# Six more fillers ahead of the first hash, and a hash of two query columns moved behind the first turns

## The chip, the cores and the metric

The kernel runs on one core of a Trainium2 chip. The core has five engines that run side by side and wait for each other by semaphores: TensorE (PE, with PEld for its weight loads), VectorE (DVE), ScalarE (ACT), GpSimd (POOL) and SyncE (SP, which issues DMAs here). TensorE writes to PSUM, which DVE and ACT read. The metric is the device time in microseconds of one execution; the median of several runs is compared.

## The reference

Hashed attention, then a gated feed-forward layer:

```python
q_bits = (np.einsum('bhsd,dk->bhsk', q, proj) > 0).astype(np.int64)
k_bits = (np.einsum('bhsd,dk->bhsk', k, proj) > 0).astype(np.int64)
q_bucket = np.sum(q_bits * powers, axis=-1)          # and k_bucket
mask = q_bucket[:, :, :, None] == k_bucket[:, :, None, :]
scores = np.where(mask, scale * np.matmul(q, k.transpose(0, 1, 3, 2)), -1000000000.0)
attn = softmax(scores)                                # over the keys
x = np.matmul(attn, v), as (4*768, 512)
out = x + sigmoid(x @ w_res) * (gelu(x @ w_gate) * (x @ w_val) @ w_out)
```

There are 4 batches of 8 heads, 768 positions, 64 dimensions, 6 hash bits, and a hidden width of 1536. A query attends only to keys in the same bucket of the 6-bit hash.

## The kernel before, in words

Two heads make a pair, so there are 16 pairs, four to a batch. A loaded pair of queries or keys is a tile of 128 partitions by 12 columns of 64 numbers; a column is a set of 128 positions, columns 0 to 5 belong to the first head and 6 to 11 to the second.

For each pair the queries and keys are prepared. `cast` (L255 to L265) writes them as bf16 into a tile `nat`, 128 wide per column: 64 values, then room for 6 bits, then a constant. `tr` (L269 to L274) transposes the loaded numbers in blocks of 32 on DVE into `t32`. For pair 0 `hash_one` (L311 to L320) multiplies `t32` by the projection, in two fp32 matmuls per call, which the profile shows as four instructions at L319; `bits_one` (L322 to L327) transposes the sums in PSUM on DVE (L324) and writes the signs as bits into `nat` (L326). `turn_pe` (L366 to L374) turns columns of `nat` by TensorE transposes into PSUM, one tile under the tag "f" for keys and one under "r" for queries, and `turned` (L376 to L382) copies them to `aug` on ACT (L380) or DVE (L382). With the bits as further rows of `aug`, one matmul gives scores that are far lower where the buckets differ.

`scores` (L494 to L513) computes a chunk of 1024 scores per partition, in a tile `sp` of the pool `sc_ps`, which has two buffers of two PSUM banks each, and takes the exponential on ACT (L512). `values` (L467 on) multiplies the exponentials with the values. A batch ends in `gate_val` and `project`, the feed-forward part, which is spread over the next batch's attention.

The order of the work in batch 0 is written out by hand in the list PLAN (L17 to L76). Lines L727 and L728 call each step in turn. Each engine carries out its own instructions in that order, and waits only for what its next instruction needs; so the list sets an order per engine, and no time. The names of steps: ('tr', pair, side, first column, last), side 0 being the queries and 1 the keys; ('hash1', ..., place); ('bits1', ...); ('turn', ..., tag); ('copy', ..., engine) is `turned`; ('S', chunk) is `scores`; ('va', pair) and ('vs', pair) prepare values on POOL; ('load', pair, side) is issued by SP; ('fill', n, columns) is `fill`.

`fill` (L227 to L229) issues matmuls of a constant into the tile `wps` (L223), whose results are used by nothing. `wps` is taken from `sc_ps` before the first score chunk. The hashes with the places 'w1' and 'w0' also use it: keys 2 to 5 in its second bank, queries 4 and 5 in its first (L313 to L315). The places 'av' are tiles of another pool. The score chunk 0 takes the other buffer of `sc_ps`, chunk 1 the one that `wps` had.

The core of the list at the place of the change, ahead of the first score chunk: fillers (4 + 44 + 4); hash of queries 0 to 3, of keys 0 and 1, of keys 2 to 5, of queries 4 and 5; turns of keys 0 and 1 and of queries 0 to 3; hash of queries 6 to 11; turns of keys 2 to 5 and of queries 4 and 5; chunk 0. Between them stand the steps of DVE, ACT and POOL.

Of the kernel before, what the change touches and what calls it, by code (L numbers as in the profile page):

```python
# [9 lines left out]
FP32 = mybir.dt.float32  # L10
# [7 lines left out]
    ('load', 1, 0), ('load', 1, 1), ('load_v', 0), ('load', 2, 0), ('load_v', 1), ('load', 2, 1),  # L18
    ('load', 3, 0), ('proj', 's', 'pssp'), ('proj', 'w', 'pppp'), ('cast', 0, 1, 'p', 0, 6),
# [73 lines left out]
def kernel(  # L93
# [17 lines left out]
    P = 128  # L111
# [37 lines left out]
    sc_ps = ctx.enter_context(tc.tile_pool(name="sc_ps", bufs=2, space=PSUM))  # L149
# [70 lines left out]
            else:  # L220
                eng.tensor_copy(dst(a), projn)

    wps = sc_ps.tile([P, 1024], FP32, tag="sp", name="wps")  # L223

    ones = nc.const_aps.tensor(1.0, [P, 1], BF16)

# [15 lines left out]
    for s in range(3):  # L242
        n = KF // 3
# [11 lines left out]
    def cast(p, side, eng, c0=0, c1=HT):  # L255
        x = (p, side)
        scale = (1.0 / C) if side == 0 else 1.0
        sl = slice(c0, c1)
        dst = nat_of(x)[:, sl, 0:D]
        if eng is nc.scalar:  # L260
            nc.scalar.activation(dst, raw[x][:, sl], AF.Copy, scale=scale)
        elif side == 0:
            eng.tensor_scalar(dst, raw[x][:, sl], scale, 1.0, op0=ALU.mult, op1=ALU.mult)  # L263
        else:
            eng.tensor_copy(dst, raw[x][:, sl])  # L265

    t32, hsum, htok = {}, {}, {}
# [43 lines left out]
    def hash_one(p, side, c0, c1, tag):  # L311
        n, x = c1 - c0, (p, side, c0)
        if tag in ("w0", "w1"):  # L313
            a = 512 * int(tag[1])
            hsum[x] = wps[:, a:a + 2 * n * 32].rearrange("p (i c n) -> p i c n", i=2, c=n)  # L315
        else:
            hsum[x] = (av_ps if tag == "av" else mm_ps).tile([P, 2, n, 32], FP32, tag=tag, name="hs1")
        for dh in range(2):
            nc.tensor.matmul(hsum[x][:, 0], projs[:, dh, :], t32[p, side][:, c0:c1, dh, :],  # L319
                             start=(dh == 0), stop=(dh == 1))  # L320
# [45 lines left out]
    def turn_pe(p, side, c0, c1, tag, pool=mm_ps):  # L366
        x = (p, side)
        if x not in aug:
            aug[x] = aug_pool.tile([P, HT, P], BF16, tag=f"aug{side}", name=f"aug{side}")
        k = (p, side, c0 // T)  # L370
        if k not in pts:
            pts[k] = pool.tile([P, T, P], BF16, tag=tag, name="pt")
        for c in range(c0, c1):
            nc.tensor.transpose(pts[k][0:KA, c % T, :], nat_of(x)[:, c, 0:KA], ident)  # L374

    def turned(p, side, c0, c1, eng):  # L376
        dst = aug[p, side][0:KA, c0:c1, :]
        pt = pts[p, side, c0 // T][0:KA, c0 % T:c0 % T + c1 - c0]
        if eng is nc.scalar:
            nc.scalar.activation(dst, pt, AF.Copy)  # L380
        else:
            eng.tensor_copy(dst, pt)  # L382
# [321 lines left out]
    def first_gv(i):  # L704
# [7 lines left out]
            [ENG[e] for e in engs]),  # L712
        cast=lambda p, side, e, *c: cast(p, side, ENG[e], *c),
        hash1=hash_one,
        bits1=bits_one,
        turn=lambda p, side, c0, c1, tag: turn_pe(p, side, c0, c1, tag, POOLS[tag]),
        copy=lambda p, side, c0, c1, e: turned(p, side, c0, c1, ENG[e]),
# [3 lines left out]
        va=vals_a, vs=vals_s, finish=finish, open=opened, preset=preset, repeat=repeat,  # L721
# [11 lines left out]
    for s in range(NSLOT, LAST):  # L733
        p, c = divmod(s, NCH)
# [60 lines left out]
```

## Time and profile before

| what | us |
|---|---|
| median of 3 runs | 341.46 |
| the three runs | 341.46, 339.53, 341.53 |
| the profiled execution's own time | 341.21 |
| its span in the trace | 339.2 |
| PE busy | 331.7 |
| DVE busy | 216.4 |
| ACT busy | 214.1 |
| POOL busy | 175.0 |

The span runs from the first to the last instruction in the trace; the execution's own time holds some 2 us more. A row of a timeline gives start, length, engine, line, operation, what is written and read, the number of instructions merged into the row, and in brackets how long the engine was idle before it and what ended that. Merged matmuls overlap, so that a row can end after the next one starts; the time from one row's start to the next one's is the better measure of pace. A row of the list of waits gives the engine and line that waited, what released it, the total in us, the number of times and the longest. The chain is the work that ended last, followed back from the end.

### The profile page before, as it was taken

The page shows a single profiled execution, that of the slowest core. Times are in us where ns is not written, and L with a number is a line of the kernel's source. Part 1 is how long each engine was busy: PE and PEld are TensorE (multiplying, and loading weights), DVE is VectorE, ACT ScalarE, POOL GpSimd, SP SyncE. Part 2 cuts the span into 40 slices and gives each one's busy share as a digit, 9 for nine tenths or more (in the row PEclk, how much of TensorE's full clock was granted, in tenths as well). Part 3 has the DMA queues.
Part 4 walks back from the last instruction along what each step waited for, and adds up shares of the span by engine and source line. Part 5 has one row for each costly group of instructions (what it writes and reads, how often), then busy time and mean ns, then how long its engine had stood idle before and what let it go on. Part 6 is the DMA issues. An engine that isn't in the chain of part 4 may idle for free.

```text
span 339.2 us, 7693 instructions
## 1 busy us (share of the span) xinstructions
PE 331.7 (98%) x3039; PEld 206.2 (61%) x3086; DVE 216.4 (64%) x458; ACT 214.1 (63%) x247; POOL 175.0 (52%) x260
## 2 busy tenths in 40 slices
PE   8999999999999999999999999999999999999996
PEld 8677665565666655555566665666565665666444
DVE  6877765656377977877477896886478444434243
ACT  4799982227999962337999983245999994322220
POOL 4579940233379962477789981667979100000000
PEclk9999999999999999999999999999999999999999
DMA  7996999999966324527057942925050340000012
GB/s 216 376 278 115 240 212 204 184 142 197 309 211 166 97 84 96 94 48 176 12 141 236 248 132 85 141 46 96 1 124 34 79 100 33 31 2 0 31 64 94
DMA packets 74387, 43.88 MB, mean 129 GB/s; under 512 B 52544, under 2 KB 71360, under 8 KB 74352
## 3 DMA queue, kind: packets, MB, share of 16 engines
q1 hardware_dynamic: 67872, 37.95, 45.0%
q0 software_dynamic: 6400, 5.44, 10.7%
q8 instruction: 24, 0.39, 0.4%
q14 instruction: 11, 0.09, 0.1%
q10 hardware_dynamic: 80, 0.00, 0.0%
HBM read 29.56 MB, written 6.29 MB: 106 GB/s over the span
## 4 chain that ended last, share of the span: by engine, by line
PE 82%; POOL 8%; ACT 4%; DVE 3%; DMA 2%; issue 2%; POOLq 0%; DVEq 0%; ACTq 0%
PE sp L526 36%; PE fps L572 14%; PE sp L501 14%; PE av L476 7%; PE rps L558 5%; POOL pr L336 4%; PE hs L284 3%; ACT ering L512 3%; PE hs L319 1%; ACT e L512 1%; PE pt L374 1%; POOL v L395 1%; DMA x_sb<-x_tok 1%; DMA ld<-in_q_dram 1%; DVE sums L342 1%
## 5 line engine op out<-in xcount | busy, mean ns | idle before, releaser
L512 ACT ACTIVATE e<-sp 128x1024 bf16<-128x1024 f32 x117 | 117.7, 1027 | 8.6 <-PE sp L501 3.5
L336 POOL TENSOR_TENSOR pr<-ld,projr 128x384 f32<-128x384 f32 x96 | 93.9, 997 | 47.1 <-DVE sums L342 32.7
L543 ACT ACTIVATE gt<-sp 128x768 bf16<-128x768 f32 x48 | 38.9, 810 | 83.7 <-PE sp L526 80.0
L501 PE MATMUL sp<-aug,aug 71*128 71x256 bf16 (+1 forms) x384 | 86.0, 326 | 0.5
L572 PE MATMUL fps<-wo,hh 128*128 128x512 bf16 (+2 forms) x287 | 74.5, 361 | 1.3
L546 DVE TENSOR_TENSOR hh<-gt,sp 128x768 bf16<-128x768 bf16 x48 | 45.8, 954 | 42.9 <-PE sp L526 39.5
L526 PE MATMUL sp<-x_sb,wg 128*128 128x512 bf16 (+1 forms) x377 | 70.6, 325 | 0.4
L526 PE MATMUL sp<-x_sb,wv 128*128 128x512 bf16 (+1 forms) x374 | 70.4, 325 | 0.5
L476 PEld LDWEIGHTS <-e 128*128 128x128 bf16 x936 | 43.6, 97 | 25.9
L342 DVE TENSOR_REDUCE sums<-pr 128x6 f32<-128x384 f32 x96 | 50.2, 542 | 10.7 <-POOL pr L336 10.4
L526 PEld LDWEIGHTS <-wg 128*128 128x128 bf16 x384 | 37.1, 98 | 25.8 <-issue 1.5
L526 PEld LDWEIGHTS <-wv 128*128 128x128 bf16 x384 | 37.5, 98 | 24.9 <-issue 0.2
L476 PE MATMUL av<-va,e 128*128 128x65 bf16 x936 | 47.0, 193 | 0.2
L572 PEld LDWEIGHTS <-hh 128*128 128x128 bf16 x312 | 28.2, 98 | 21.5
L501 PEld LDWEIGHTS <-aug 71*128 71x128 bf16 x384 | 29.3, 97 | 11.5 <-issue 2.7
L575 DVE SCALAR_TENSOR_TENSOR fps<-th,fps 128x512 f32<-128x512 f32 (+2 forms) x26 | 17.0, 653 | 25.9 <-PE fps L572 25.8
L512 ACT ACTIVATE ering<-sp 128x1024 bf16<-128x1024 f32 x27 | 25.8, 1031 | 1.7 <-PE sp L501 1.4
L558 PE MATMUL rps<-wr,x_sb 128*128 128x512 bf16 x91 | 26.0, 379 | 0.2
L562 ACT ACTIVATE th<-rps 128x512 f32<-128x512 f32 x24 | 14.3, 594 | 18.7 <-PE rps L558 17.5
L273 DVE STREAM_TRANSPOSE t<-ld 128x768 f32<-128x768 f32 (+3 forms) x28 | 23.0, 842 | 0.8 <-PE hs L284 0.6
L455 DVE COPY av<-av 128x390 f32<-128x390 f32 x24 | 13.6, 566 | 14.6 <-PE av L451 14.5
L263 POOL TENSOR_SCALAR nat<-ld 128x768 bf16<-128x768 f32 (+1 forms) x12 | 9.6, 805 | 19.1 <-DMA aug<-nat 17.2
(72 smaller groups left out, 261.7 us busy)
## 6 DMA issues: line engine op xcount, KB each, us to landing
ldv<-in_v_dram SPq DMA_DIRECT2D x16, 384.0 KB, 5.4
out_dram<-o SPq DMA_DIRECT2D x23, 256.0 KB, 2.1
ld<-in_q_dram SPq DMA_DIRECT2D x15, 384.0 KB, 6.2
ld<-in_k_dram SPq DMA_DIRECT2D x15, 384.0 KB, 5.5
wg<-in_moe_w_gate_dram POOLq DMA_DIRECT2D x4, 384.0 KB, 8.6
wv<-in_moe_w_val_dram POOLq DMA_DIRECT2D x4, 384.0 KB, 10.1
wo<-in_moe_w_out_dram POOLq DMA_DIRECT2D x3, 512.0 KB, 7.2
wr<-in_moe_w_res_dram POOLq DMA_DIRECT2D x1, 512.0 KB, 15.5
```

Of the source, the lines that this page charges most:

```text
L273: nc.vector.transpose(t32[p, side][:, sl].rearrange("p c h n -> p (c h n)"), raw[p, side][:, sl].rearrange("p c d -> p (c d)"))
L336: nc.gpsimd.tensor_mul(pr, raw[x][:, hi * T:(hi + 1) * T], projr[:, bit].unsqueeze(1).to_broadcast([P, T, D]))
L342: nc.vector.reduce_sum(sums[x][:, hi * T:(hi + 1) * T, bit], pr, axis=mybir.AxisListType.X)
L476: nc.tensor.matmul(av[p, hi][:, qt, :], e[:, off:off + P], va[:, hi, jt, 0:D + 1], start=first, stop=(repeats(p, hi) and jt == T - 1), ski ...
L501: nc.tensor.matmul(sp[:, off:off + nq * P], ks[0:KA, hi * T + jt, :], qs[0:KA, hi * T + qt0:hi * T + qt0 + nq, :], start=True, stop=True)
L512: nc.scalar.activation(e, sp, AF.Exp, scale=float(ALPHA))
L526: nc.tensor.matmul(sp[:, c0:c1], w[:, kk, bass.ts(m, P)], xs[:, kk, c0:c1], start=(kk == 0), stop=(kk == KM - 1))
L543: nc.scalar.activation(gt, sp[:, 0:S], AF.Gelu)
L546: nc.vector.tensor_mul(hidden[b][:, m, :], gt, ps[1][:, 0:S])
L558: nc.tensor.matmul(rps, x_sb[b][:, kk, t, :], wr[:, kk, :], start=(kk == 0), stop=(kk == KM - 1))
L572: nc.tensor.matmul(fps[:, cs], hh[:, m, bass.ts(t, P)], wo[:, m, cs], start=(m == 0), stop=(m == KF - 1))
L575: nc.vector.scalar_tensor_tensor(fps[:, cs], th[:, cs], 1.0, fps[:, cs], op0=ALU.add, op1=ALU.mult)
```

## The change

Three things change. The second group of fillers has 50 instead of 44. The pool `sc_ps` gives a second tile `wpt` beside `wps`, and the hash of keys 2 to 5 ('w1') now stands at the beginning of `wps`, that of queries 4 and 5 ('w0') at the beginning of `wpt`; score chunk 0 then takes the buffer of `wps` and chunk 1 that of `wpt`. And in the list, the hash of queries 4 and 5 stands behind the first two turns instead of ahead of them. On each of DVE, ACT, POOL and SP the order of instructions is the same as before.

```diff
-    ... ('tr', 0, 0, 4, 6), ('fill', 44, 64),
+    ... ('tr', 0, 0, 4, 6), ('fill', 50, 64),
...
-    ('hash1', 0, 1, 2, 6, 'w1'), ('hash1', 0, 0, 4, 6, 'w0'), ('tr', 0, 0, 6, 12),
-    ('turn', 0, 1, 0, 2, 'f'), ('copy', 0, 1, 0, 2, 's'), ('bits1', 0, 1, 2, 6), ('load', 3, 1),
-    ('bits1', 0, 0, 4, 6), ('turn', 0, 0, 0, 4, 'r'), ('va', 0), ('tr', 0, 1, 6, 12),
+    ('hash1', 0, 1, 2, 6, 'w1'), ('tr', 0, 0, 6, 12), ('bits1', 0, 1, 2, 6),
+    ('turn', 0, 1, 0, 2, 'f'), ('copy', 0, 1, 0, 2, 's'), ('turn', 0, 0, 0, 4, 'r'), ('hash1', 0, 0, 4, 6, 'w0'), ('load', 3, 1),
+    ('bits1', 0, 0, 4, 6), ('va', 0), ('tr', 0, 1, 6, 12),
...
-    wps = sc_ps.tile([P, 1024], FP32, tag="sp", name="wps")
+    wps, wpt = [sc_ps.tile([P, 1024], FP32, tag="sp", name=name) for name in ("wps", "wpt")]
...
-            a = 512 * int(tag[1])
-            hsum[x] = wps[:, a:a + 2 * n * 32].rearrange("p (i c n) -> p i c n", i=2, c=n)
+            hsum[x] = (wpt, wps)[int(tag[1])][:, 0:2 * n * 32].rearrange("p (i c n) -> p i c n", i=2, c=n)
```

2 rows, old and new, of the table PLAN are left out of this document.

## The prediction

> **What bounds the kernel now.** I read the page first (busy time, chain), then the chain in order of time over the first 50 us, then the timelines of PE, PEld, DVE and ACT over the first 12 us with shapes kept apart, and last the waits from 10.5 us on.
>
> ```profile
> span 339.2 us, 7693 instructions
> ...
> PE 331.7 (98%) x3039; PEld 206.2 (61%) x3086; DVE 216.4 (64%) x458; ACT 214.1 (63%) x247; POOL 175.0 (52%) x260
> ...
> PE 82%; POOL 8%; ACT 4%; DVE 3%; DMA 2%; issue 2%; POOLq 0%; DVEq 0%; ACTq 0%
> ```
>
> PE is busy for 98% of the span and carries 82% of the chain. Work that moves off PE's way near the start moves the end only if PE, and what follows it closely, comes out earlier. So the question is when PE finishes the preparation of pair 0. The chain says what that stretch is made of (start, length, what):
>
> ```profile
> 3.42 0.46 DVE t L273
> 3.88 0.14 issue
> 4.01 1.94 PE hs L319 x8
> 5.95 1.71 PE wps L319 x8
> 7.66 0.64 PE pt L374 x6
> 8.30 1.35 PE hs L319 x4
> 9.64 0.34 PE pt L374 x6
> ```
>
> From 4.01 us on there is nothing but PE in it, back to back. The reader should compare the two rows of six transposes: the same instructions take 0.64 us, then 0.34 us. PE's own timeline shows the same for other forms:
>
> ```profile
> 0.85 2.93 PE L229 MATMUL wps<-const-bfloat16-1.0 128*128 128x64 bf16 x52 [0.85 <-PEq L779]
> 4.01 1.94 PE L319 MATMUL hs<-t,projs 128*128 128x128 f32 x8 [0.24 <-DVE t L273]
> 5.74 1.92 PE L319 MATMUL wps<-t,projs 128*128 128x128 f32 x8
> 7.45 0.85 PE L374 MATMUL pt<-ident,nat 128*71 128x128 bf16 x6
> 8.09 1.55 PE L319 MATMUL hs<-t,projs 128*128 128x192 f32 x4
> 9.48 0.50 PE L374 MATMUL pt<-ident,nat 128*71 128x128 bf16 x6
> 9.82 1.23 PE L501 MATMUL sp<-aug,aug 71*128 71x512 bf16 x5
> 10.88 0.81 PE L319 MATMUL hs<-t,projs 128*128 128x192 f32 x4
> 11.53 0.50 PE L374 MATMUL pt<-ident,nat 128*71 128x128 bf16 x6
> ```
>
> Start to start (next row's start less this one's), four 192-column hash matmuls take 9.48 - 8.09 = 1.39 us and later 11.53 - 10.88 = 0.65; six transposes 8.09 - 7.45 = 0.64 and later 9.82 - 9.48 = 0.34. So PE goes at half pace until about 9.48 and at full pace from there. The page's PEclk reads 9 throughout and does not show it; the rows do. There is one break before: PE waits 0.24 us for DVE's first transpose, ahead of 4.01.
>
> **The change, part by part.**
>
> *Six more fillers.* Their weight loads and the next one's:
>
> ```profile
> 0.81 2.80 PEld L229 LDWEIGHTS <-const-bfloat16-1.0 128*128 128x128 bf16 x52 [0.81 <-issue]
> 3.98 1.78 PEld L319 LDWEIGHTS hs<-t,projs 128*128 128x128 f32 x8 [0.37 <-POOL projs L221]
> ```
>
> 52 in 2.80 us is 0.054 each; six are 0.32 us. PEld is idle for 0.37 us before 3.98. The last filler's load then ends at 0.81 + 2.80 + 0.32 = 3.93, ahead of 3.98, so the first hash should start where it does: cost 0, cover the 0.37 us of waiting for DVE's transpose. If that cover shrinks (the first half of the queries landing earlier), at most the whole 0.32 us goes onto the path. The six close the break on PE nearly completely (0.05 us is left).
>
> *The two hashes get a buffer each.* DVE's timeline (its own order is the same after the change, so are those of ACT, POOL and SP's loads: of the moved steps only the hash and the turns are PE's, and they change places with each other):
>
> ```profile
> 5.99 0.27 DVE L324 STREAM_TRANSPOSE hs<-hs 128x64 f32<-128x64 f32 x1 [0.20 <-PE hs L319]
> 6.29 0.17 DVE L326 TENSOR_SCALAR nat<-hs 128x12 bf16<-128x12 f32 x1
> 6.38 0.57 DVE L273 STREAM_TRANSPOSE t<-ld 128x384 f32<-128x384 f32 x1
> 7.70 0.33 DVE L324 STREAM_TRANSPOSE wps<-wps 128x128 f32<-128x128 f32 x1 [0.75 <-PE wps L319]
> 8.06 0.18 DVE L326 TENSOR_SCALAR nat<-wps 128x24 bf16<-128x24 f32 x1
> 8.28 0.27 DVE L324 STREAM_TRANSPOSE wps<-wps 128x64 f32<-128x64 f32 x1
> 8.58 0.17 DVE L326 TENSOR_SCALAR nat<-wps 128x12 bf16<-128x12 f32 x1
> 8.67 0.57 DVE L273 STREAM_TRANSPOSE t<-ld 128x384 f32<-128x384 f32 x1
> 9.98 0.42 DVE L382 COPY aug<-pt 71x512 bf16<-71x512 bf16 x1 [0.75 <-PE pt L374]
> ```
>
> The bits of keys 2 to 5 (7.70) wait 0.75 us until all eight matmuls into wps are done (5.74 + 1.92 = 7.66), though their own four come first. With a tile of their own they can start when DVE is free, 6.38 + 0.57 = 6.95. But who waits for them? The turn of keys 2 to 5, at 9.48, that is 1.24 us after 8.06 + 0.18 = 8.24. At the pace of before this gain is worth nothing on the path.
>
> *The hash of queries 4 and 5 behind six transposes.* Nothing is added, PE's work only changes order. The turns of keys 0, 1 need the bits that end at 6.29 + 0.17 = 6.46; PE finishes its third hash's issue near 6.6 (half of the 1.71 us between 5.74 and 7.45), so no wait at the old pace. The hash ends 0.64 us later, at 8.30; bits 8.28 to 8.75 take 0.47, so they end at 8.8; their turn follows four transposes behind 9.48: a margin of 0.7 us, covered by the 1.39 us hash of columns 6 to 11. Cost 0; without that cover 0.47 us and more. The second score buffer is taken until 8.8, and the second score chunk wants it after 10 us: no wait. Each queue that steps are moved past (SP's load of pair 3's keys, POOL's values of pair 0) keeps its order.
>
> *What is left is the pace.* PE went to full pace after 9.48 - 4.01 = 5.47 us of unbroken work; the fillers before the break did not bring it. If it is unbroken work that counts, and the break is closed, the count starts at 0.85 and full pace comes at 0.85 + 5.47 = 6.3 us. Then, in the new order: rest of the third hash to 6.55; six transposes 0.34, to 6.9; the moved hash at half of its 0.86, to 7.3; columns 6 to 11, 0.65, to 8.0; six transposes, to 8.3: first scores at about 8.35 instead of 9.82, 1.45 us earlier. DVE has to keep up: the moved hash's last result stands at about 7.6, its bits at 8.1, needed at 8.2 by the last two transposes: just in time. In the old order and tile these would stand the same 0.1 us from the edge, so the reorder adds little by itself. DVE next does 0.57 us of transposing, to 8.67, then the copy that stood at 9.98: 1.3 us earlier.
>
> I take that the time is kept to the end, less a little: DVE's 1.3 and PE's 1.45 bound it from below and above at this turning point, and an earlier one (right at the first hash, 4.0) saves up to half of 9.48 - 4.0, cut by DVE's chain (rows 5.99 to 8.75, work of 0.27 + 0.17 + 0.57 + 0.33 + 0.18 + 0.27 + 0.17, that PE's clock does not shorten) to about 2. [...]
>
> What could be late next is data. From 10.5 to 50 us the list of waits, 17 entries, begins
>
> ```profile
> POOL nat L305 <- DVE ht L296: 4.3, 2, 2.5
> DVE rec L420 <- PE av L448: 3.8, 1, 3.8
> DVE aug L382 <- PE pt L374: 2.5, 2, 2.0
> ```
>
> and names no DMA at all: no engine waits there for a load. One load is tight before it:
>
> ```profile
> 9.66 0.82 POOL L387 CAST va<-ldv 128x768 bf16<-128x768 f32 x1 [1.29 <-DMA ldv<-in_v_dram]
> ...
> 15.42 0.65 PE L476 MATMUL av<-va,ering 128*128 128x65 bf16 x16
> ```
>
> It does not move, but its first reader, at 15.42, has 4.9 us to spare after 10.48. So I take the whole gain as kept.
>
> The sum: fillers 0, buffers 0, reorder 0, pace -1.3 to -2.0, I take -1.55, a little beyond the two figures at 6.3 since some executions will turn earlier. The profiled execution took 341.21 us (span 339.2 and 2.0 around it), 0.25 under the median of 341.46; against its own time 339.7, against the median 339.9. The three runs before are 341.46, 339.53 and 341.53: one of them already stands 1.9 us under the others, which is what an earlier turn of the pace would look like. I read it so, but no trace of that run is there.
>
> **Rivals.**
>
> *The pace turns when it did.* The break of 0.24 us may not be what decides: what counts could be how densely PE is filled, and the first hashes may be too thin whatever stands ahead of them. Then only the hidden reorderings remain: 341.4 us, 341.2 to 341.6. For it: 2.93 us of fillers alone had not raised the pace. Against it: the stretch from 5.74 to 9.48 is made of the same kinds of hash and of transposes, and at its end the pace rose. [...]
>
> *More than that.* Keys 2 to 5 being free 0.75 us earlier matters more at full pace than I reckon, and the turn comes near 4.3 in most runs: 2.4 us, 339.0. Against: the same chain of DVE.
>
> *Slower: the fillers hold up the first hash.* Place: PE between last filler and first hash. By the rows 0.05 us are left. Once DVE's transpose ends more than 0.05 us sooner than 3.42 + 0.46 = 3.88, each filler stands in the way; the price is at most 0.32 us, on the path one to one, with the pace turning as late as before: 341.8 us. It decides where that transpose starts before about 3.37 us.
>
> **How the numbers follow.** The earlier turn 0.62 (339.9, own range 339.3 to 340.4), no earlier turn 0.20 (341.4), more 0.08 (339.0), slower 0.10 (341.8). The predicted time is that of the first. The range takes in the other cases with some 0.4 us of scatter below: 338.6 to 341.9. A measurement of this kernel can tell about 1% from no change, 3.4 us: under 338.05 or over 344.87. No case reaches either: half the slow stretch is 2.7 us at the very most, and the fillers cost 0.3. I leave 0.03 on the fast and 0.04 on the slow side for something unseen, such as a wait that the new order brings; 0.93 for within 1%.
>
> **What would show it.** Right: 58 fillers ending near 3.93, no idle row before the first hash, which still starts near 4.0; the first six transposes already at about 0.05 us each; DVE's 128x128 transpose of wps at about 6.95 with no wait for the later hash; first scores near 8.4 and the first exponential 1.4 us earlier than 10.45:
>
> ```profile
> 10.45 3.99 ACT L512 ACTIVATE ering<-sp 128x1024 bf16<-128x1024 f32 x4
> ```
>
> Wrong: transposes still at 0.107 us each before 9 us (no earlier turn), the first hash near 4.3 (held up), PE idle before the turns, or a load that becomes the end of a wait between 8 and 25 us (gain given back).

## The result and the profile after

Over 22 runs each the changed kernel takes 340.96 us (340.35 to 341.74) and the kernel before 339.49 us (338.97 to 341.53): ratio of the means 1.0033, interval 1.0021 to 1.0046. The change makes it slower, by a third of a per cent (the medians differ by 0.43%). The forecast was 339.9 us, a gain.

One thing about the base has to be said first. Of the three runs of before that were known, 341.46, 339.53 and 341.53, two belong to the slower of two groups, and so does the profiled one, 341.21. All 138 runs of its code that were taken here fall into two groups (one of 345.95 is left out): 94 at 338.67 to 340.04, 44 at 341.01 to 341.59. The first group is called the usual kind below, the second the later kind; the trace of before is of the later kind.

The page of the changed kernel shows six matmuls and six weight loads more, and a span 0.6 us shorter than that of the trace of before. The last line is one of the DMA queues: packets, MB, share.

```profile
span 338.6 us, 7705 instructions
...
PE 329.7 (97%) x3045; PEld 203.9 (60%) x3092; DVE 216.3 (64%) x458; ACT 213.8 (63%) x247; POOL 175.3 (52%) x260
...
q8 instruction: 24, 0.39, 0.5%
```

PE's timeline at the start (one line number less than before throughout):

```profile
0.85 3.25 PE L229 MATMUL wps<-const-bfloat16-1.0 128*128 128x64 bf16 x58 [0.85 <-PEq L778]
3.98 1.11 PE L318 MATMUL hs<-t,projs 128*128 128x128 f32 x8
4.92 0.66 PE L318 MATMUL wps<-t,projs 128*128 128x128 f32 x4
5.80 0.50 PE L373 MATMUL pt<-ident,nat 128*71 128x128 bf16 x6 [0.21 <-DVE nat L325]
6.13 0.61 PE L318 MATMUL wpt<-t,projs 128*128 128x64 f32 x4
6.58 0.87 PE L318 MATMUL hs<-t,projs 128*128 128x192 f32 x4
7.30 0.76 PE L373 MATMUL pt<-ident,nat 128*71 128x128 bf16 x6
7.89 1.23 PE L500 MATMUL sp<-aug,aug 71*128 71x512 bf16 x5
```

There is no break ahead of the first hash any more, it starts at 3.98 as before (4.01), and full pace is there from the first hash on: six transposes take 6.13 - 5.80 = 0.33 us, where the first six of before took 0.64. The first scores stand at 7.89 instead of 9.82. DVE's rows show the hash of keys 2 to 5 released by itself, at 6.07, instead of at 7.70 after the later hash; and PE now waits 0.21 us ahead of the turns, for the bits of keys 0 and 1, with the moved hash queued behind them.

```profile
5.48 0.17 DVE L325 TENSOR_SCALAR nat<-hs 128x12 bf16<-128x12 f32 x1
5.57 0.58 DVE L273 STREAM_TRANSPOSE t<-ld 128x384 f32<-128x384 f32 x1
6.07 0.29 DVE L323 STREAM_TRANSPOSE wps<-wps 128x128 f32<-128x128 f32 x1
```

So the start is 1.93 us earlier than in the trace of before. Set side by side, the exponentials keep 1.93 us until 110 us and 1.90 until the end of batch 1. Three of the last ones there, before and after:

```profile
119.48 3.25 ACT L512 ACTIVATE e<-sp 128x1024 bf16<-128x1024 f32 x3
```

```profile
117.58 3.25 ACT L511 ACTIVATE e<-sp 128x1024 bf16<-128x1024 f32 x3
```

Then comes the feed-forward part of batch 1. PE's first matmuls that need the last part of `x_sb`, before and after:

```profile
128.48 0.48 PE L526 MATMUL sp<-x_sb,wg 128*128 128x512 bf16 x2
```

```profile
127.90 0.48 PE L525 MATMUL sp<-x_sb,wg 128*128 128x512 bf16 x2 [1.37 <-DMA x_sb<-x_tok]
```

Of the 1.90 us, 0.58 are left, and they stay 0.55 to 0.58 to the end. PE waits 1.37 us for the DMA that transposes `x_tok`. SP's rows for the store ahead of it and for the transpose, before and after:

```profile
125.00 0.36 SPq L580 DMA_DIRECT2D out_dram<-o  x1
125.70 1.21 SPq L429 DMA_TRANSPOSE x_sb<-x_tok  x1
```

```profile
123.13 0.35 SPq L579 DMA_DIRECT2D out_dram<-o  x1
123.82 2.27 SPq L428 DMA_TRANSPOSE x_sb<-x_tok  x1
```

Times of landings and of single packets stand in the trace, not in the views shown. By the landings the store took 127.16 - 123.13 = 4.03 us instead of 2.06, the transpose 127.86 - 123.82 = 4.04 instead of 2.74. No load runs beside them. Busy time in three stretches of after (the last two numbers are the DMA share and GB/s):

```profile
122.00:123.00 1.00, 1.00 (x7) 0.59 (x6) 0.96 (x2) 0.98 (x2) 0.55 (x1) 1.00 0.00 0
...
125.00:126.00 1.00, 1.00 (x7) 0.45 (x5) 0.00 (x0) 0.00 (x0) 0.00 (x0) 1.00 2.34 132
126.00:127.00 1.00, 0.53 (x3) 0.13 (x2) 0.36 (x1) 0.00 (x0) 0.00 (x0) 1.00 0.08 22
```

Ahead of the store nothing moves (0 GB/s); from 125 to 126 us the packets stand waiting (a share of 2.34 at 132 GB/s), and from 126 to 127 hardly anything moves, though the transpose is not done. One packet is there that belongs to no transfer of the program. Queue q8 carries instructions, 0.39 MB in 24 packets of 16 KB each; it is taken for PE's, since PE has 6137 of the 7705 instructions (matmuls and weight loads) and the next engine on the page, DVE, has 458. One of its packets starts at 124.04 and takes 1.59 us, to 125.63. In the trace of before the same packet, the eleventh, starts at 129.41, when the transpose has landed (128.44).

The trace also shows what the packet holds back. Of the store's 128 packets of 2 KB, 120 have started by 124.71; the last eight, a sixteenth, follow one behind the other from 125.61 to 126.65, the first as the fetch ends. The landing of each of the two is told by sixteen updates of a semaphore: of the store's, fifteen come 1.87 to 2.04 us after its issue, as before (1.90 to 2.06), and one at 4.03. The transpose then lands late as a whole, all sixteen at 3.88 to 4.04. So the fetch stands in the way of one sixteenth of the store, which fits one of the 16 DMA engines that the page counts.

The question for the experiments was whether the six fillers, as twelve more instructions, have moved this fetch.

### The profile page after: what moved, and what is told of

Same layout as the page of the kernel before. It is cut to its first block, busy times and chain, and to the rows that moved or that the text cites. A ratio compares the mean times of both kernels' runs of the same rounds, so it can differ in the third digit from the quotient of the medians.

```text
span 338.6 us, 7705 instructions
## 1 busy us (share of the span) xinstructions
PE 329.7 (97%) x3045; PEld 203.9 (60%) x3092; DVE 216.3 (64%) x458; ACT 213.8 (63%) x247; POOL 175.3 (52%) x260
## 4 chain that ended last, share of the span: by engine, by line
PE 82%; POOL 8%; ACT 4%; DVE 3%; issue 2%; DMA 1%; POOLq 0%; DVEq 0%; ACTq 0%
PE sp L525 36%; PE fps L571 14%; PE sp L500 14%; PE av L475 7%; PE rps L557 5%; POOL pr L335 4%; PE hs L284 3%; ACT ering L511 3%; DMA x_sb<-x_tok 1%; ACT e L511 1%; PE wps L229 1%; PE pt L373 1%; POOL v L394 1%; DVE sums L341 1%; POOL va L386 1%
```

## The experiments

In all of them the theory called F is: the number of PE's instructions ahead of that place sets where the fetch falls, and a fetch among the packets of the store and the transpose costs about 1.4 us. The rivals are named with each. Each kernel ran 12 times beside 35 runs of before on the same chip; the kernels of one group share them. "Filled" means that the fillers take the time of the changed kernel's 58, so that there is no break.

**First group: which part of the change makes the loss** (before: 339.42 us)

*e1, before again.* No edit.

> The kernel before, unchanged, for a trace of its usual execution. The 22 runs of before show two groups, 18 from 338.97 to 339.98 us and 4 from 341.15 to 341.53; the trace on hand (341.21) is of the second. If the groups are the two times at which PE comes to full pace, this trace, if it is of the first group, has its first score matmul near 8 us instead of 9.82, ends near 339.4, and its x_sb transpose at the end of batch 1 lands in 2.7 us after issue as in the trace on hand, with no wait of PE for it.

Measured: 339.49 us, 338.94 to 341.59, 5 of 12 over 341. Its trace is again of the later kind (first scores at 9.75, no wait for the transpose), so no trace of before's usual execution is on record. The two groups stand: medians 339.33 and 341.34 of the 138 runs.

*e2, fillers only.*

```diff
-('fill', 44, 64)
+('fill', 50, 64)
```

> The kernel before with 50 fillers in place of 44 in the second group and nothing else. Theory F (fetch): twelve more PE instructions move the place in the program at which PE's next 16 KB of instructions are fetched by DMA; at the end of batch 1 this fetch falls into the store and transpose that PE waits for, 1.4 us. It expects 340.8 to 341.1 us, a wait of PE for DMA x_sb of over 1 us near 126 us, and no run above 341.8. Rival R (order): the new order of hash and turns and the earlier start make the loss; it expects 339.2 to 339.5 us here and no such wait.

Measured: 340.93 us, ratio 1.0023 (1.0003 to 1.0043). SP's two rows and PE's wait:

```profile
123.72 0.35 SPq L580 DMA_DIRECT2D out_dram<-o  x1
124.41 1.76 SPq L429 DMA_TRANSPOSE x_sb<-x_tok  x1
```

```profile
128.00 0.48 PE L526 MATMUL sp<-x_sb,wg 128*128 128x512 bf16 x2 [0.88 <-DMA x_sb<-x_tok]
```

The fillers alone make the whole loss, in the old order; the rival that blames the order falls. The wait is 0.88 us, a little under the 1 us expected. The fetch started at 124.76, 1.04 us after the store was issued.

*e3, order and buffers only.*

```diff
-('fill', 50, 64)
+('fill', 44, 64)
```

(against the changed kernel)

> The changed kernel with 44 fillers as before. Theory F: the number of PE instructions is that of before, so the fetch stays where it was: 339.2 to 339.6 us, with some runs near 341.2 where PE comes to full pace late. Rival R: 340.8 to 341.1, with the wait for DMA x_sb.

Measured: 339.68 us, ratio 0.9992 (0.9970 to 1.0014), 2 of 12 runs over 341; no wait, the fetch 5.08 us after the store. The median is 0.08 over the range expected. The order and the second buffer give nothing that can be told from no change. This trace has the 44 fillers and a break of 0.33 us, and yet it is of the usual kind: the first scores stand at 8.23.

*e4, the time of the fillers without their number.*

```diff
-('fill', 50, 64)
+('fill', 38, 64), ('fill', 6, 128)
```

> The changed kernel with the time of its fillers but the number of instructions of before: 38 of 64 columns and 6 of 128 columns in place of 50 of 64. Theory F: no wait for DMA x_sb, 339.0 to 339.4 us and no run over 340.2, since the break ahead of the first hash is closed too. Rival R, and a rival by which it is the filled break itself that costs: 340.8 to 341.1.

Measured: 339.67 us, ratio 0.9988 (0.9969 to 1.0007), and all 12 runs between 339.19 and 340.05. SP's rows are those of before again:

```profile
123.33 0.35 SPq L579 DMA_DIRECT2D out_dram<-o  x1
124.03 1.21 SPq L428 DMA_TRANSPOSE x_sb<-x_tok  x1
```

The same PE time in six fewer fillers loses nothing. So the loss hangs on the count of instructions, and the filled break does what it is for: the group over 341 is gone. The median was expected at 339.0 to 339.4 and is 0.3 above that.

**Second group: moving the fetch** (before: 340.04 us, since 16 of its 35 runs here were of the later kind and one took 345.95)

Against this mixed base the ratios of e6, e7 and e8 are 1.0010 (0.9992 to 1.0029), 1.0017 (0.9992 to 1.0043) and 1.0012 (0.9992 to 1.0032), which by themselves show no loss. It is read against e5 and against the usual kind of before instead.

*e5, the old order with the fillers of e4.* The edit of e4 in before's list, where 44 stood.

> The kernel before in its order and buffers, with the wide fillers of e4 (38 of 64 columns, 6 of 128): break filled, number of PE instructions as before. Theory F: no wait for DMA x_sb, 339.3 to 339.9 us like e4, and no run near 341.3, so the order and the second buffer are worth nothing once PE is at full pace. Rival O: the moved hash is worth something of its own; then this is 0.3 us or more over e4's 339.67.

Measured: 339.40 us, 338.80 to 339.74, ratio 0.9981 (0.9959 to 1.0003), no wait. As expected; the rival that gives the order a worth of its own falls (e5 is 0.27 us under e4, though on another chip).

*e6, 24 instructions more than before.*

```diff
-('fill', 50, 64)
+('fill', 44, 64), ('fill', 12, 32)
```

> The changed kernel with 44 fillers of 64 columns and 12 of 32 in its second group: the same columns, but 24 PE instructions more than before instead of 12. Theory F: the fetch at the end of batch 1, which stood at 127.9 us with none more and at 124.0 with 12 more, moves on to about 120.5, ahead of the store at 123.1: no wait for DMA x_sb there, 339.4 to 340.0 us, unless another fetch now hits another transfer. Rival N (any added instruction, or any longer filler group, costs): 340.9 us or more.

Measured: 340.69 us, 340.31 to 341.39, so every run is above all of e5's. F's number was wrong: the loss is still there, and so is the wait.

```profile
123.51 0.35 SPq L579 DMA_DIRECT2D out_dram<-o  x1
124.20 2.23 SPq L428 DMA_TRANSPOSE x_sb<-x_tok  x1
```

```profile
128.25 0.48 PE L525 MATMUL sp<-x_sb,wg 128*128 128x512 bf16 x2 [1.32 <-DMA x_sb<-x_tok]
```

But the fetch had not moved on to 120.5: it started at 124.52, 1.01 us after the store, just as with 12 more. So the fetch does not shift evenly with the count. That leaves F's link between fetch and loss, and takes away its arithmetic.

*e7, the same count, added later.* Ahead of chunk 8's scores of pair 0, in `scores`; the real matmuls overwrite the result.

```diff
+for _ in range(6 if (p, c) == (0, 8) else 0):
+    nc.tensor.matmul(sp[:, 0:1], ks[0:KA, 0, :], qs[0:KA, 0, 0:1], start=True, stop=True)
```

> The kernel before with six one-column matmuls added ahead of the scores of chunk 8 of pair 0, whose real matmuls overwrite what these write: 12 PE instructions more, but after the start. Theory F: 340.6 to 341.2 us for most runs, some near 342.7 where PE comes to full pace late, and the wait of PE for DMA x_sb at the end of batch 1. Rival S (the loss comes from the early start or from the fillers themselves): 339.4 to 339.8 and some near 341.5, no such wait.

Measured: 340.86 us, 8 runs from 339.93 to 341.09 and 4 from 342.04 to 343.35, with medians 340.56 and 342.83 where before's two kinds have 339.33 and 341.34. The trace is of the latter, with a wait of 1.6 us for the transpose and the fetch 1.00 us after the store. As expected: the break is not touched here, the start is that of before, and the loss comes with the twelve instructions alone.

*e8, 6 instructions more.*

```diff
-('fill', 50, 64)
+('fill', 44, 64), ('fill', 3, 128)
```

> The changed kernel with 44 fillers of 64 columns and 3 of 128 in its second group: the same columns, 6 PE instructions more than before instead of 12. Theory F: the fetch falls between 124.0 and 127.9, near 126, where the transpose's packets are nearly all through: a wait of 0 to 1 us, 339.5 to 340.6 us, between e4 and the changed kernel. Rival N: 340.3, half of the loss, by count alone.

Measured: 340.81 us, over both expectations. PE waits 1.32 us; the fetch started at 125.25, 2.16 us after the store, amid the transpose's packets, which landed 4.01 us after issue instead of 2.74. The place was within F's stretch, if earlier than its 126; the price was not what F said: all of it, not a part.

**Third group: past the transfer, or without it** (before: 339.44 us)

*e9, 48 instructions more.*

```diff
-('fill', 50, 64)
+('fill', 32, 64), ('fill', 36, 32)
```

> The changed kernel with 32 fillers of 64 columns and 36 of 32: the same columns, 48 PE instructions more than before. [...] F mended (the fetch comes in a burst, the packets of the store and the transpose behind it are what is delayed) expects that 48 more bring it ahead of that burst: the fetch well before the store, no wait of PE for DMA x_sb over 0.5 us, 339.4 to 340.1 us. Rival N (any more instructions than before cost, wherever the fetch falls): 340.6 us or more.

Measured: 339.49 us, 339.01 to 340.06, ratio 0.9998 (0.9984 to 1.0012). The fetch started at 122.69, 1.15 us ahead of the store, and was done (1.06 us) before the store's packets:

```profile
123.84 0.36 SPq L579 DMA_DIRECT2D out_dram<-o  x1
124.54 1.21 SPq L428 DMA_TRANSPOSE x_sb<-x_tok  x1
```

Four times as many instructions added as in the change, and no loss. This is the run that tells most: not the number costs, but where the fetch falls. That the fetch comes in a burst, as F mended has it, is not shown: in the traces of before and after the 24 packets of q8 stand singly, 6.5 us or more from start to start.

*e10, the transpose without DMA.* The changed kernel, with 50 fillers; for batch 1 the last transposes go to PE, and their DMA is not issued.

```diff
-elif hi == 1 and (b > 0 or hp < XDMA) and not (b in XJOIN and hp == 0):
+elif hi == 1 and (b > 0 or hp < XDMA) and not (b in XJOIN and hp == 0) and not (b == 1 and hp == HP - 1):
...
             if b < B - 1:
+                if b == 1:
+                    x_turn(b, HP - 1)
                 mlp_mm(NMM)
```

> The changed kernel with the last transpose of batch 1 made by six PE transposes and two copies in place of the DMA that the fetch falls into; the 50 fillers stay. F: the fetch still comes near 124 us, but PE no longer waits for a DMA there: 1.4 us less, 0.35 us of transposes more, 339.7 to 340.1 us. Rival P (PE itself runs out of instructions at that place, the late transpose only goes with it): PE is idle near 126 us all the same, 341.0 us or more.

Measured: 340.22 us, ratio 1.0015 (0.9997 to 1.0033). PE's rows at the place:

```profile
124.45 0.51 PE L459 MATMUL pt<-ident,x_tok 128*128 128x128 bf16 x6
124.80 2.75 PE L571 MATMUL fps<-wo,hh 128*128 128x512 bf16 x12
127.39 0.49 PE L525 MATMUL sp<-x_sb,wg 128*128 128x512 bf16 x2
```

No idle time, though the fetch started at 125.55, in the midst. So PE does not run out of instructions there; it waited for the transpose and for nothing else, and rival P falls. Against the trace of e4 this one is 0.43 us behind ahead of the place (122.46 and 122.03) and 0.59 after it (127.39 and 126.80), so the place costs 0.16 instead of the changed kernel's 1.3. It costs less than the 0.35 us of the six transposes because the DMA transpose has no slack even undisturbed: in e4 it lands at 126.76 and PE goes on at 126.80, with 2.82 us from the start of the twelve matmuls ahead, where e10 needs 2.59. The median is 0.1 over the range expected; where that comes from was not pursued.

*e11 and e12, 12 instructions fewer, in the new and the old order.*

```diff
-('fill', 50, 64)      (e11; in e12 the 44 of before)
+('fill', 26, 64), ('fill', 12, 128)
```

> The changed kernel with 26 fillers of 64 columns and 12 of 128: the same columns, 12 PE instructions fewer than before. F: the fetch comes later than in e4, past the transpose: no wait, 339.3 to 339.8 us, no run near 341.3. Rival M (any move of the fetch off the place it had before costs): 340.6 or more.

> The order and buffers of before with the fillers of e11, on the same chip as e11: what the order and the second buffer are worth at full pace with the break filled. F: within 0.15 us of e11. Rival O: the order is worth 0.3 us or more, so e11 is lower by that.

Measured: 339.70 us (339.04 to 339.98), ratio 0.9996 (0.9980 to 1.0012), and 339.37 us (338.69 to 340.03), ratio 0.9984 (0.9965 to 1.0002). No wait in either, the fetch 4.6 and 4.5 us after the store. With twelve fewer the fetch comes hardly later than in e4 (4.5). The new order is not lower but 0.3 us higher by the medians, more than the 0.15 expected and on the other side than its worth would be.

Put together, by instructions more than before, each in its own trace (e10 has no such transpose):

| more | kernels | fetch after the store's issue, us | transpose lands after its issue, us | PE waits, us | median, us |
|---|---|---|---|---|---|
| -12 | e11, e12 | 4.6, 4.5 | 2.74, 2.74 | none | 339.70, 339.37 |
| 0 | e3, e4, e5 | 5.1, 4.5, 4.4 | 2.74, 2.73, 2.73 | none | 339.68, 339.67, 339.40 |
| 6 | e8 | 2.16 | 4.01 | 1.32 | 340.81 |
| 12 | changed, e2 | 0.91, 1.04 | 4.04, 3.55 | 1.37, 0.88 | 340.96, 340.93 |
| 12, added later | e7 | 1.00 | 4.32 | 1.6 | 340.86 |
| 24 | e6 | 1.01 | 4.01 | 1.32 | 340.69 |
| 48 | e9 | -1.15 | 2.75 | none | 339.49 |

In the traces where the fetch starts 0.9 to 2.2 us after the store's issue, PE waits, and the kernel takes 1.2 to 1.5 us more than before's 339.49. Where it starts 1.15 us ahead of the store, or 4.4 us and more behind it, when the transpose has landed, the list of waits has no such wait and nothing is lost. Starts between 2.2 and 4.4 us were not measured. "None" does not mean slack: in before the transpose lands at 128.44 and PE's matmul starts at 128.48, in e9 at 127.29 and 127.33, so a delay of the transpose reaches PE in full.

That the fetch delays the two transfers is shown by the table and by the landings: as in the changed kernel, fifteen of the store's sixteen updates come by 2.05 us after issue in e2, e6 and e7 and one comes late (at 3.55, 4.00 and 4.34), and in every trace with the fetch clear all sixteen come by 2.06. In e8, whose fetch starts when the store is nearly through, the late one comes at 2.67, and the transpose is held up all the same. That PE's loss is the wait for the transpose and nothing else is shown by e10. Why all of the transpose waits when a sixteenth of the store is late was not pursued.

No kernel here is clearly below before. e5 and e12, the old order with the break filled by fewer, wider fillers, come nearest: their intervals reach 1.0003 and 1.0002. What the filled break brings is that the later kind is gone: in the 60 runs of the five kernels with a filled break and the fetch clear (e4, e5, e9, e11, e12) none took over 340.06 us, where 44 of 138 took over 341 before.

## Why the prediction was wrong

*The fillers fit into the break and cost nothing on PE.* Right: the hash starts at 3.98 behind 58 of them, with no idle time between.

*Full pace comes earlier, at 6.3, and the first scores at 8.35.* Right in kind, mis-sized: 4.0 and 7.89 in the profiled execution, between 3.7 and 6.7 in the other traces with a filled break. The 5.47 us of unbroken work that the count rested on is no constant: from the first filler to the rise it is 4.04 - 0.85 = 3.19 us in the changed kernel. The step from the two figures to -1.55, for executions that turn earlier, rested on no trace of before; in place of it the traces with a filled break show the rise at 3.7 to 6.7 us. The gain at the start, 1.93 us in the trace, lies within the 1.3 to 2.0 of the sum's pace term; but the bound of about 2 was not worked out there (it names 1.96 us of DVE's work and no step from it to a saving), so that the two are close is luck.

*Order and buffers are worth 0.* Right within what can be told (e3), with a loss rather than a gain at full pace: in the changed kernel PE waits 0.21 us ahead of the turns, as the hash that would have filled this time stands behind them. I had reckoned that the bits at 6.46 are no wait "at the old pace" and did not ask again at the new. e11 and e12 fit a loss of 0.2 to 0.3 us, and so do two traces at nearly the same pace: e6 in the new order has full pace from 5.71 and its first scores at 8.32, e5 in the old order from 5.95 and 8.16. They do not settle it. The margin of 0.7 us for the turn of queries 4 and 5 is 0.9 by the prediction's own rows, since four transposes of 0.057 us come first; nothing hung on it.

*The median is the base.* "Against the median 339.9" failed: I read the run at 339.53 as one with an earlier pace, but took it for the exception. By their times, 94 of 138 of before's executions have the early start already, so the gain of 1.9 us was to be had in one third only, some 0.6 us in the mean and nothing in the median. No trace of such a run of before exists; that they are early starts is read from the gap of 2.0 us between the two kinds and from e3's trace. That two of the three known runs were late was bad luck.

*"So I take the whole gain as kept."* This is the step that turned the sign. The gain held for 120 us, and then 1.32 us were lost in one wait that ended at 127.90, as the transpose landed 4.04 us after issue instead of 2.74. I looked for waits on loads up to 50 us, and not for the transfers on which PE hangs later; and I counted the twelve added instructions by their time on PE alone, not by their place in the stream that PE fetches.

*The rivals.* None was it. The slower one, fillers holding up the first hash, did not happen. The first one did not happen either; whether density counts was not tested. That the time would stay within 1% was right. That 340.96 lies within the stated range is luck: none of the cases it was made of has this cause.

## What to carry to other kernels

Time that is filled with instructions is not free if the count moves an instruction fetch onto a transfer that the bottleneck engine waits for (here 1.3 us); where a change adds instructions, look at the few transfers with no slack. Fillers of another width can take the same time with the count unchanged (e4, 339.67 us), and a larger count can be harmless too (e9, 339.49 us); only the trace tells which. Three runs of a kernel with two groups of times are no base: ask for more, or see which group the trace belongs to. A gain at the start should be followed through the trace to every later point at which the bottleneck engine has less slack than a transfer might lose.

## What the runs showed of the hardware

Queue q8, which by the page carries instructions, moves 0.39 MB in 24 packets of 16 KB, each 0.9 to 1.9 us long in the traces of before and after. In the changed kernel one of them, 1.59 us long, holds back one sixteenth of a store by 2.0 us (4.03 us from issue to landing instead of 2.06) and a whole transpose by 1.3 (4.04 instead of 2.74). PE's own supply of instructions shows no loss by it: in e10, with the fetch at 125.55 and no transfer to wait for, PE has no idle time at the place. Where the fetch meets the transfer that PE waits for, in the changed kernel, it costs 1.3 us of 340.

The fetch does not move evenly with the count: 6 more instructions bring it 2.3 us forward against the store (4.5 to 2.16), 12 and 24 more 3.5 us alike, 48 more 5.6. What holds it at 1.0 us is open.

The times of one program fall into two kinds: 94 of before's 138 executions have a median of 339.33 us and 44 one of 341.34, which is read as two times at which PE comes to full pace. The clock records in the traces raise the pace at 9.47 and 9.40 us in the two traces of before, at 4.04 in the changed kernel, at 5.29 in e3 and at 6.68 in e2. The break ahead of the first hash alone does not decide: e3's, of 0.33 us, has the rise at 5.29 behind it, before's, of 0.24, has it at 9.47. With the break filled and the fetch clear none of 60 runs was of the later kind. What does decide was not shown.
